# A spectral mixing and SwiGLU kernel: smaller n tiles, three a tiles for four, and a last step of 21 units

## The chip, the core and the metric

The kernel runs on one core of a Trainium2 chip. The core has five engines that run side by side: TensorE (PE in the profile; its weight loads are shown apart as PEld), VectorE (DVE), ScalarE (ACT), GpSimd (POOL) and SyncE (SP), which here only issues DMA transfers. Each engine works through its own instructions in order and waits on semaphores for the others. Matmul results land in PSUM, eight banks of 128 x 512 fp32; everything else lives in SBUF or in DRAM. The metric is the time of one execution on the device in microseconds, as the median of several runs.

## What is computed

For each of 8 batches of 3008 rows with 256 channels, a Fourier filter along the rows, then a normalisation and a gated feed-forward layer on every row:

```
def _attn_ref(x, filt_r, filt_i):
    X = np.fft.rfft(x, axis=1)
    F = (filt_r + 1j * filt_i)[None, :, :]
    y = np.fft.irfft(X * F, n=x.shape[1], axis=1)
    return y.astype(np.float32)

def _moe_ref(x, w_gate, w_val, w_out, rms_g):
    rms = np.sqrt(np.mean(x * x, axis=-1, keepdims=True) + 1e-06)
    xn = x / rms * rms_g
    g = xn @ w_gate
    silu = g * (1.0 / (1.0 + np.exp(-g)))
    return (silu * (xn @ w_val) @ w_out).astype(np.float32)
```

Here d_ff is 1536. The feed-forward layer holds most of the arithmetic: 24,064 rows times three matrices of 256 x 1536.

## The kernel before

**Two kinds of work.** The row index of a batch is split as 94 x 32, and the Fourier transform and its inverse are done as matmuls in three stages with layout changes through DRAM between them. For a batch b these are: `load_x`; `s1` (16 pieces i, each a matmul into PSUM `psa` and a copy into the tile `a_sb`; every four pieces fill one a tile of 8 rows, which SyncE writes to `a_tmp`, line 153); `load_a2`; `s2` and `s2z` (12 pieces j: filter and second transform, tiles `z_sb`, written to `z_tmp`); `load_z2`; and the last step, 16 pieces q of two rows each. A piece q of the last step is `s3` (a matmul into `psy`, and two squares with a sum on ScalarE, line 256), `s3r` (two operations on GpSimd that give rho, the factor 1/rms, lines 265 and 267) and `s3n` (VectorE multiplies the PSUM result by rho into the tile `n_sb`, line 276). Every four pieces fill one n tile of 8 rows, which SyncE writes to `n_tmp` (line 280). Then `load_xn` reads n back transposed, one chunk of up to 512 rows at a time, by transposing DMAs on SyncE (line 318). A chunk takes rows from all n tiles of its batch, so its read waits for all writes of n.

The feed-forward layer is cut in units. A unit is one chunk of rows and one of twelve blocks of 128 hidden channels: two matmuls for the gate (`pg`, line 341), two for the value (`pv`, line 345), a silu on ScalarE (`sg`, line 348) and a product on VectorE (`hh`, line 350). `project` follows three units behind and adds the output matmuls into `po` (line 364); after the twelfth block it copies `po` out and SyncE writes it (line 381 in batch 0, line 389 later). Batch 0 has 8 chunks of 376 rows, units 0 to 95; each later batch has 6 chunks, 72 units.

**The order.** It is written out by hand. `plan` holds, for each unit number (slot), which pieces are issued right after that unit's matmuls, those of `s3n` first, then `s3r`, `s2z` and the rest (line 469); after them comes `project` of three units before. So the transform of batch b runs inside the units of the batch before it. For each batch `o_s3` is the slot of the first piece of the last step: 63 for batch 1, and 31 units ahead of the batch's own units for the others. Piece q is in slot `o_s3 + q + q // 2` for batch 1 and `o_s3 + q + q // 4` for the others; its `s3r` is one slot later, its `s3n` two. The six `load_xn` of a batch start three slots after the last `s3`. For batch 1 that puts `s3` of q = 15 in slot 85, its `s3n` in slot 87 and the first `load_xn` in slot 88; unit 96 is the first that uses it.

**Before unit 0.** The transform of batch 0 goes another way (`s1_first`, `turn`, no a tile), and the part ahead of the units ends as follows (lines 568 to 588): SyncE loads the first half of z of batch 0 and four pieces of the weights; `s1` of batch 1 runs its pieces 0 to 11, whose copies alternate between ScalarE and VectorE; then come four matmuls and eight squares of `s3` for batch 0, and pieces 12 to 15 of `s1`, all four copied by VectorE (line 151); then `s3n_first(0)`, in which VectorE scales the first rows of n (line 287), and `turn_n`, which transposes them on TensorE and evicts them into `xn`, so that unit 0 can start. On VectorE the order is thus: the four copies of pieces 12 to 15, then the scalings.

**Tiles and buffers.** A tile with a tag takes the next of `bufs` buffers, and the first instruction that writes it waits until all users of that buffer's earlier tile are done, DMA writes included. `a_sb` has four buffers of 8 x 256 fp16 per partition, `n_sb` two of the same size. PSUM is one pool of eight banks for all stages.

Of the kernel before, what the change touches and what calls it, by code (L numbers as in the profile page):

```python
# [11 lines left out]
FP16 = mybir.dt.float16  # L12
# [5 lines left out]
D = 256  # L18
# [7 lines left out]
PY = 96  # L26
QZ = 4 * NS
# [47 lines left out]
def kernel(  # L75
# [11 lines left out]
    nc = tc.nc  # L87
# [10 lines left out]
    n_dram = nc.dram_tensor("n_tmp", (B, PY, RP, D), FP16, kind="Internal").ap()  # L98
    n0_dram = nc.dram_tensor("n0_tmp", (RP // 4, PY, 4, D), FP16, kind="Internal").ap()

    glob = ctx.enter_context(tc.tile_pool(name="glob", bufs=1))
    work = ctx.enter_context(tc.tile_pool(name="work", bufs=2))
    psum = ctx.enter_context(tc.tile_pool(name="psum", bufs=8, space=bass.MemoryType.PSUM))

    def bank(name):
        return psum.tile([P, 512], FP32, tag="bank", name=name)
# [32 lines left out]
    def s1(b, i, eng):  # L139
        v = st[b]  # L140
        if i % 4 == 0:
            v.a = work.tile([QZ, 8, D], FP16, tag="a_sb", name="a_sb", bufs=4)
        ps = bank("psa")
        nc.tensor.matmul(ps[0:QZ, :], w1_sb, v.x[i // 4][:, ds(2 * (i % 4), 2), :],  # L144
                         start=True, stop=True)
        dst = v.a[:, ds(2 * (i % 4), 2), :]
        src = ps[0:QZ, :].rearrange("p (r d) -> p r d", r=2)
        if eng == 0:
            nc.scalar.activation(out=dst, in_=src, func=AXT.Copy)  # L149
        else:  # L150
            nc.vector.tensor_copy(out=dst, in_=src)
        if i % 4 == 3:
            nc.sync.dma_start(
                a_dram[b].rearrange("s c r d -> (s c) r d")[:, ds(8 * (i // 4), 8), :], v.a)
# [116 lines left out]
    def s3n(b, q):  # L271
        v = st[b]
        ps, rho = v.y.pop(q)
        if q % 4 == 0:
            v.n = work.tile([PY, 8, D], FP16, tag="n_sb", name="n_sb", bufs=2)
        nc.vector.tensor_tensor(out=v.n[:, ds(2 * (q % 4), 2), :],  # L276
                                in0=ps[0:PY, :].rearrange("p (r d) -> p r d", r=2),
                                in1=rho.unsqueeze(-1).to_broadcast([PY, 2, D]), op=ALU.mult)
        if q % 4 == 3:
            nc.sync.dma_start(n_dram[b, :, ds(8 * (q // 4), 8), :], v.n)  # L280

    def s3n_first(c):
        v = st[0]
        n = work.tile([PY, 8, D], FP16, tag="n_sb", name="n0", bufs=2)
        for k in range(2):
            ps, rho = v.y.pop(2 * c + k)
            nc.vector.tensor_tensor(out=n[:, ts(k, 2), :],
                                    in0=ps[0:PY, :].rearrange("p (r d) -> p r d", r=2),
                                    in1=rho.unsqueeze(-1).to_broadcast([PY, 2, D]), op=ALU.mult)
        if c >= PRE:  # L290
            nc.sync.dma_start(n0_dram[c], n[:, 0:4, :])
        return n

    def turn_n(c, n):
# [141 lines left out]
    def at(slot, f, *args):  # L436
        plan.setdefault(slot, []).append((f, args))

    for c in range(PRE, RP // 4):
        k = 2 + 8 * (c - PRE)  # L440
        at(k, s3, 0, 2 * c, 2)
        at(k + 1, s3, 0, 2 * c + 1, 2)
        at(k + 2, s3r, 0, 2 * c, 2)
        at(k + 4, s3n_first, c)
        at(k + 7, load_xn_first, c)

    for b in range(1, B):
        end = FIRST + UNITS * (b - 1)
        o_s1 = 44 if b == 2 else end - 118
        o_s2, p_s2 = (14, 3) if b == 1 else (end - 75, 2)  # L450
        o_s3 = 63 if b == 1 else end - 31
        if b > 1:
            at(o_s1 - 18, load_x, b)
            for i in range(16):
                at(o_s1 + i, s1, b, i, i % 2 if b == 2 else 0)
            at(o_s1 + 16, load_a2, b)
        for j in range(12):
            k = o_s2 + p_s2 * j
            at(k, s2, b, j)
            at(k + (3 if b < 2 else 5), s2z, b, j)  # L460
        at(k + (4 if b < 2 else 6), load_z2, b)
        for q in range(16):
            k = o_s3 + q + (q // 2 if b == 1 else q // 4)
            at(k, s3, b, q)
            at(k + 1, s3r, b, q)
            at(k + 2, s3n, b, q)
        for c in range(6):
            at(k + 3 + c, load_xn, b, c)
# [62 lines left out]
    with tc.manual_schedule():  # L531
# [40 lines left out]
        for i in range(12):  # L572
            s1(1, i, i % 2)
# [4 lines left out]
        for i in range(12, 16):  # L578
            s1(1, i, 1)
        load_wo(1)  # L580
        load_wo(2)
        n0 = s3n_first(0)
        turn_n(0, n0)
        load_w(4)
        n1 = s3n_first(1)
        at(2, turn_n, 1, n1)
        load_z2(0, 16, 16)
# [44 lines left out]
```

## Time and profile before

| | us |
|---|---|
| median of 3 runs | 901.75 (901.72 to 901.91) |
| the profiled execution | 903.26 |
| its span, first to last instruction | 901.4 |
| VectorE busy | 646.3 |
| ScalarE busy | 640.3 |
| GpSimd busy | 336.5 |

The profile is of one execution. Its times are in microseconds from the first instruction. A row of the timeline gives the start, the length, engine, line, operation, the tiles written and read, the shapes and how many were merged; in brackets stands how long the engine was idle before, and what ended that. A row of the chain of waits gives start, length and what the end of the kernel was waiting for then. Rows of SyncE (SPq) are issues of DMAs, not the transfers; for these the profile has the time from issue to landing. A row of windows gives, for a stretch, its length, how long each engine was busy with how many instructions, the clock that TensorE was granted as a share of full speed, the busy share of the DMA engines and the data rate. Matmul ends are modelled, so matmuls that follow each other overlap in the rows.

### The profile page before, as it was taken

The numbers are of one execution on the slowest core, as the hardware profiler recorded it, in microseconds if no ns is written. First come the engines' busy times: TensorE is split into PE (matmuls) and PEld (weight loads), VectorE is DVE, ScalarE is ACT, GpSimd is POOL, SyncE is SP. The second block draws the span as 40 slices with busy tenths as digits, with TensorE's granted clock in tenths as the row PEclk, the third lists the DMA queues.
The fourth block names the chain that finished last, engine by engine and source line by source line (L and its number), as shares of the span: only waits on it lengthen the run. The fifth ranks groups of instructions, "written<-read, shape, count | busy, mean of one in ns | idle before, by whom it ended". The sixth has DMA issues, their size and how long they took to land.

```text
span 901.4 us, 16402 instructions
## 1 busy us (share of the span) xinstructions
PE 865.6 (96%) x5528; PEld 550.1 (61%) x5528; DVE 646.3 (72%) x1026; ACT 640.3 (71%) x1455; POOL 336.5 (37%) x438
## 2 busy tenths in 40 slices
PE   5669999999999999999999999999999999999998
PEld 4336776666556655666556665566656666565565
DVE  4668887796578947797477965789467985865554
ACT  5556768687886778677886878867786775854543
POOL 3822104492245803285044921459033750400000
PEclk9769999999999999999999999999999999999999
DMA  8996675465436555344655554365553425250111
GB/s 205 239 265 148 163 162 184 114 151 132 140 100 142 133 147 168 97 110 129 164 147 128 134 127 147 111 131 145 146 159 96 101 76 118 77 130 24 35 37 45
DMA packets 140812, 117.30 MB, mean 130 GB/s; under 512 B 53976, under 2 KB 125272, under 8 KB 140728
## 3 DMA queue, kind: packets, MB, share of 16 engines
q1 hardware_dynamic: 136248, 102.13, 42.2%
q0 software_dynamic: 4240, 13.90, 8.7%
q8 instruction: 43, 0.70, 0.3%
q14 instruction: 41, 0.34, 0.1%
q10 hardware_dynamic: 240, 0.23, 0.1%
HBM read 56.96 MB, written 60.42 MB: 130 GB/s over the span
## 4 chain that ended last, share of the span: by engine, by line
PE 85%; DMA 5%; ACT 4%; DVE 2%; issue 2%; POOL 1%; SPq 0%; DVEq 0%; ACTq 0%; POOLq 0%
PE po L364 25%; PE pv L345 25%; PE pg L341 25%; PE psy L250 3%; ACT junk L256 2%; PE psa L144 2%; PE psz L229 2%; PE psp L200 2%; DMA z<-z_tmp 2%; ACT sg L348 1%; DMA w_sb<-w0tab 1%; DMA z_tmp<-z_sb 1%; DVE t L208 1%; DMA fr_sb<-in_filt_r_dram 1%; DMA n_tmp<-n_sb 0%
## 5 line engine op out<-in xcount | busy, mean ns | idle before, releaser
L350 DVE TENSOR_TENSOR hh<-pv,sg 128x512 f16<-128x512 f32 (+2 forms) x600 | 393.3, 658 | 221.3 <-ACT sg L348 129.8
L348 ACT ACTIVATE sg<-pg 128x512 f32<-128x512 f32 (+2 forms) x600 | 341.0, 568 | 198.4 <-PE pg L341 161.4
L364 PE MATMUL po<-wo_sb,hh 128*128 128x256 f16 (+1 forms) x2288 | 347.9, 272 | 0.2 <-DVE n_sb L276 0.2
L345 PE MATMUL pv<-xn,wv_sb 128*128 128x512 f16 (+2 forms) x1200 | 343.0, 367 | 4.6 <-ACT sg L348 3.8
L341 PE MATMUL pg<-xn,wg_sb 128*128 128x512 f16 (+2 forms) x1200 | 343.1, 367 | 3.1 <-DMA xn<-n_tmp 1.9
L364 PEld LDWEIGHTS <-hh 128*128 128x128 f16 (+1 forms) x2288 | 233.2, 104 | 102.7 <-DVE n_sb L276 0.5
L345 PEld LDWEIGHTS <-wv_sb 128*128 128x128 f16 x1200 | 117.5, 98 | 133.5 <-issue 6.6
L265 POOL TENSOR_SCALAR me<-ms 96x2 f32<-96x2 f32 (+1 forms) x120 | 26.1, 217 | 347.3 <-ACT junk L256 340.3
L341 PEld LDWEIGHTS <-wg_sb 128*128 128x128 f16 x1200 | 117.4, 98 | 16.8 <-DMA xn<-n_tmp 2.1
L217 POOL TENSOR_TENSOR pi<-pi,fi_sb 64x512 f32<-64x512 f32 x72 | 91.2, 1267 | 71.3 <-ACT pi L214 67.8
L256 ACT ACTIVATE junk<-psy 96x256 f16<-96x256 f32 x256 | 97.0, 379 | 20.6 <-PE psy L250 8.6
L218 POOL TENSOR_TENSOR qq<-pr,pi 128x512 f16<-128x512 f32 x72 | 91.6, 1272 | 10.6 <-DVE pi L216 5.0
L267 POOL TENSOR_TENSOR rho<-me,half_sb 96x2 f32<-96x2 f32 (+1 forms) x120 | 87.5, 729 | 10.0
L276 DVE TENSOR_TENSOR n_sb<-psy,rho 96x512 f16<-96x512 f32 x112 | 75.8, 677 | 0.0
L234 ACT ACTIVATE z_sb<-psz 128x512 f16<-128x512 f32 x96 | 57.3, 597 | 10.2 <-PE psz L232 5.9
L149 ACT ACTIVATE a_sb<-psa 96x512 f16<-96x512 f32 x94 | 55.6, 591 | 7.1 <-PE psa L144 3.4
L250 PE MATMUL psy<-z,t_sb 96*96 96x512 f16 x128 | 49.5, 391 | 6.8 <-DMA z<-z_tmp 6.8
L216 DVE TENSOR_TENSOR pi<-psp,fi_sb 64x512 f32<-64x512 f32 x72 | 49.9, 693 | 1.9
L215 DVE TENSOR_TENSOR pr<-psp,fr_sb 128x512 f32<-128x512 f32 x72 | 49.6, 689 | 0.7
L256 ACT ACTIVATION_READ_ACCUMULATOR junk<-psy 96x1 f32 x256 | 49.0, 191 | 0.0
L214 ACT ACTIVATE pi<-psp 64x512 f32<-64x512 f32 x72 | 42.4, 588 | 6.1
L144 PE MATMUL psa<-xt,w_sb 94*96 94x512 f16 x112 | 44.2, 417 | 1.6 <-DMA xt<-in_x_dram 1.6
(57 smaller groups left out, 386.7 us busy)
## 6 DMA issues: line engine op xcount, KB each, us to landing
out_dram<-o SPq DMA_DIRECT2D x70, 256.0 KB, 2.5
z_tmp<-z_sb SPq DMA_DIRECT2D x32, 384.0 KB, 2.3
xt<-in_x_dram POOLq DMA_DIRECT2D x32, 376.0 KB, 7.2
a_tmp<-a_sb SPq DMA_DIRECT2D x28, 384.0 KB, 3.6
a<-a_tmp SPq DMA_DIRECT2D x28, 384.0 KB, 5.8
z<-z_tmp SPq DMA_DIRECT2D x7, 1536.0 KB, 10.0
n_tmp<-n_sb SPq DMA_DIRECT2D x28, 384.0 KB, 3.0
out_dram<-o SPq DMA_DIRECT2D x12, 224.0 KB, 2.6
```

Source lines behind the costliest of these rows:

```text
L144: nc.tensor.matmul(ps[0:QZ, :], w1_sb, v.x[i // 4][:, ds(2 * (i % 4), 2), :], start=True, stop=True)
L217: nc.gpsimd.tensor_tensor(out=pi[64:P], in0=pi[64:P], in1=fi[64:P], op=ALU.mult)
L218: nc.gpsimd.tensor_tensor(out=qq, in0=pr, in1=pi, op=ALU.subtract)
L250: nc.tensor.matmul(ps[0:PY, :], t_sb, v.z2[:, ts(q, 2), :], start=True, stop=True)
L256: nc.scalar.activation(out=junk, in_=ps[0:PY, ts(i, D)], func=AXT.Square, scale=0.0625, accum_out=v.ms[:, ds(k + i, 1)])
L267: nc.gpsimd.tensor_tensor(out=rho, in0=me, in1=half_sb[:, 0:2 * pair], op=ALU.pow)
L276: nc.vector.tensor_tensor(out=v.n[:, ds(2 * (q % 4), 2), :], in0=ps[0:PY, :].rearrange("p (r d) -> p r d", r=2), in1=rho.unsqueeze(-1).to_ ...
L341: nc.tensor.matmul(pg[:, 0:w], wg_sb[:, dt_, ts(jt, P)], xn[:, dt_, 0:w], start=(dt_ == 0), stop=(dt_ == 1))
L345: nc.tensor.matmul(pv[:, 0:w], wv_sb[:, dt_, ts(jt, P)], xn[:, dt_, 0:w], start=(dt_ == 0), stop=(dt_ == 1))
L348: nc.scalar.activation(out=sg[:, 0:w], in_=pg[:, 0:w], func=AXT.Silu)
L350: nc.vector.tensor_tensor(out=hh[:, 0:w], in0=pv[:, 0:w], in1=sg[:, 0:w], op=ALU.mult)
L364: nc.tensor.matmul(po[0:n, ts(0 if alone else s4 % 2, D)], hh[:, ds(s4 * wb, n)], wo_sb[:, jt, :], start=(jt == 0 and (s4 % 2 == 0 or alone)),
```

## The change

Three edits. The tag `n_sb` gets six buffers of four rows in place of two of eight: a tile is allocated at every second piece q and written to DRAM after the next one, so a batch issues eight writes of 192 KB in place of four of 384 KB; batch 0's own n tile has four rows, all used. The tag `a_sb` gets three buffers in place of four, so that a batch's fourth a tile takes a buffer that has been used three tiles earlier. The SBUF taken by both together stays the same (12 KB and 12 KB per partition in place of 8 and 16). And the sixteen pieces of batch 1's last step have one free slot after every third in place of every second: slots 63 to 83 in place of 63 to 85, with `s3r`, `s3n`, the writes of n and the six `load_xn` moved with them (first `load_xn` in slot 86 in place of 88).

```diff
@@ s1
-            v.a = work.tile([QZ, 8, D], FP16, tag="a_sb", name="a_sb", bufs=4)
+            v.a = work.tile([QZ, 8, D], FP16, tag="a_sb", name="a_sb", bufs=3)
@@ s3n
-        if q % 4 == 0:
-            v.n = work.tile([PY, 8, D], FP16, tag="n_sb", name="n_sb", bufs=2)
-        nc.vector.tensor_tensor(out=v.n[:, ds(2 * (q % 4), 2), :],
+        if q % 2 == 0:
+            v.n = work.tile([PY, 4, D], FP16, tag="n_sb", name="n_sb", bufs=6)
+        nc.vector.tensor_tensor(out=v.n[:, ds(2 * (q % 2), 2), :],
...
-        if q % 4 == 3:
-            nc.sync.dma_start(n_dram[b, :, ds(8 * (q // 4), 8), :], v.n)
+        if q % 2 == 1:
+            nc.sync.dma_start(n_dram[b, :, ds(4 * (q // 2), 4), :], v.n)
@@ s3n_first
-        n = work.tile([PY, 8, D], FP16, tag="n_sb", name="n0", bufs=2)
+        n = work.tile([PY, 4, D], FP16, tag="n_sb", name="n0", bufs=6)
...
-            nc.sync.dma_start(n0_dram[c], n[:, 0:4, :])
+            nc.sync.dma_start(n0_dram[c], n)
@@ the plan
-            k = o_s3 + q + (q // 2 if b == 1 else q // 4)
+            k = o_s3 + q + q // (3 if b == 1 else 4)
```

## The prediction

> **What bounds the kernel now.** I read the busy times first, then who waits for whom, then the chain of waits around the two places that the change touches, and last the timeline there, engine by engine.
>
> ```profile
> PE 865.6 (96%) x5528; PEld 550.1 (61%) x5528; DVE 646.3 (72%) x1026; ACT 640.3 (71%) x1455; POOL 336.5 (37%) x438
> ```
>
> TensorE (PE) is busy for 865.6 of 901.4 us. So only 36 us of the span are open to a change of order, and any later start of the feed-forward part is paid almost in full, because after it TensorE hardly pauses. The view of waits, of which two rows matter here, says where it does:
>
> ```profile
> PE pv L345 <- ACT sg L348: 3.8, 5, 0.8
> ...
> PE pg L341 <- DMA xn<-n_tmp: 1.9, 1, 1.9
> ```
>
> The second is one wait of 1.9 us: the first unit of the second batch (unit 96) wants the transposed n of that batch. The chain of waits shows its pieces (start, length, what), and the timeline of TensorE the idle time in brackets:
>
> ```profile
> 167.51 4.16 DMA n_tmp<-n_sb
> ...
> 171.75 3.65 DMA xn<-n_tmp
> ```
> ```profile
> 175.45 0.61 PE L341 MATMUL pg<-xn,wg_sb 128*128 128x512 f16 x2 [1.85 <-DMA xn<-n_tmp]
> ```
>
> The last write of n to DRAM (4.16 us, issued once VectorE has scaled its rows), the transposing read (3.65 us), then TensorE, idle for 1.85 us. TensorE would have been ready at 175.45 - 1.85 = 173.60. That idle time is what the shorter step (21 units for 24) can win. The other place is the start of the feed-forward part. These are rows of SyncE's queue, of the DMA issued there, of VectorE, GpSimd and TensorE:
>
> ```profile
> 46.86 7.23 SPq L153 DMA_DIRECT2D a_tmp<-a_sb  x4
> ```
> ```profile
> L153 SPq DMA_DIRECT2D a_tmp<-a_sb x1: 652/652/652, 46.9 to 46.9; - x1
> ...
> DMA to landing us min/median/max: 7.2/7.2/7.2
> ```
> ```profile
> 51.27 2.48 DVE L151 CAST a_sb<-psa 96x512 f16<-96x512 f32 x4 [8.15 <-PE psa L144]
> 53.68 1.27 DVE L287 TENSOR_TENSOR n<-psy,rho 96x512 f16<-96x512 f32 x2
> ```
> ```profile
> 51.95 1.05 POOL L267 TENSOR_TENSOR rho<-me,half_sb 96x4 f32<-96x4 f32 x1
> ```
> ```profile
> 56.46 0.79 PE L341 MATMUL pg<-xn,wg_sb 128*128 128x376 f16 x2 [0.79 <-ACT xn L304]
> ```
>
> VectorE copies the second batch's fourth a tile (four casts from 51.27), then at once scales the first n (53.68), whose factor rho was ready at 51.95 + 1.05 = 53.00. From there runs the path to unit 0: transposes of n on TensorE, their eviction by ScalarE (xn, the releaser in the last row), first matmul at 56.46. So the four casts stand directly ahead of the critical path, without slack: n starts when they end.
>
> **The change part by part.** *Three a tiles in place of four.* The second batch is the first to use a tiles (batch 0 goes another way), so its fourth tile is a new buffer before and the first tile's buffer after. The first cast into it must then wait until the write of that first tile has left it. That write was issued at 46.86, behind the z loads and four weight loads on SyncE, and landed 7.2 us later, at 54.06. The DMAs ahead of it on SyncE and the casts that feed them are untouched by the change, so the cast starts at 54.06 in place of 51.27: **+2.79 us**. Behind it on VectorE stand the three other casts and the two scalings of n; for these wait the transposes, ScalarE's eviction and unit 0, all with no cover. On SyncE the write of the fourth tile, four weight loads, one z load and the loads of a stand behind those casts and start as much later, as do the units that use them; I count nothing more for them. Bounds: a release that takes as long to be seen as the one from landing to transposing read in the chain (171.75 - 167.51 - 4.16 = 0.08) adds 0.1, the rounding of 7.2 takes or adds 0.05. I take 2.79, from 2.7 to 2.9; that there is no wait at all is a rival below.
>
> The clock then decides what the later start costs. The windows view of TensorE (stretch, length, busy, granted clock, DMA share, GB/s):
>
> ```profile
> 48.70:52.12 3.42, 3.23 (x8) 0.50 1.02 328
> ...
> 55.53:58.95 3.42, 2.63 (x11) 0.50 0.93 241
> 58.95:62.36 3.41, 3.41 (x18) 0.50 1.01 217
> 62.36:65.77 3.41, 3.41 (x27) 1.00 1.15 234
> ```
>
> Unit 0 runs at half clock, and full clock is granted at 62.36, after the first stretch that is wholly busy; 3.23 of 3.42 at 48.70 was not enough. After the change unit 0 starts at 56.46 + 2.79 = 59.25, inside the stretch 58.95 to 62.36, which is then about 3.1 busy, less than the 3.23 that failed. If stretches lie where they did, the clock rises one later, at 65.77: the half-clock part lasts 65.77 - 59.25 = 6.52 in place of 62.36 - 56.46 = 5.90 us, and half of the 0.62 is lost: +0.3. I take +0.2, from 0 (small waits of TensorE just behind may swallow it) to 0.3. The Trainium skill (TensorE: Matmul & The Clock Gate, Part 1: The HAM clock gate) says that the clock rises after a busy window of about 3.4 us, and that these windows run freely, unaligned to the kernel. By its free-running grid alone, the next edge inside the run being enough, the clock would still rise at 62.36 here; this is the first rival below.
>
> Later batches use the three tiles too. There the first tile is written nine units ahead of the fourth tile's first copy. The tile's view gives the slowest write of a from the third batch on (215 to 665 us), the list of DMAs the median of all, and of the 192 KB writes of n in the first batch:
>
> ```profile
> DMA to landing us min/median/max: 3.0/4.5/7.9
> ```
>
> ```profile
> a_tmp<-a_sb SPq DMA_DIRECT2D x28, 384.0 KB, 3.6
> ...
> n_tmp<-n SPq DMA_DIRECT2D x6, 192.0 KB, 2.2
> ```
>
> No unit is shorter than 0.97 us (rows below), so nine are 8.7 us, against 7.9 at most and 3.6 in the median: no wait. If that cover were gone, ScalarE's copies would be held for the remainder of a write, 7.9 us at worst, and TensorE for what its banks don't cover.
>
> *The second batch's last step in 21 units.* The sixteen steps q start at unit 63 + q + q/3 in place of 63 + q + q/2, so the last scaling moves from unit 87 to 85 and the first transposing read from 88 to 86. The pace of TensorE, the lag of VectorE and what else stood on SyncE:
>
> ```profile
> 159.70 0.48 PE L341 MATMUL pg<-xn,wg_sb 128*128 128x376 f16 x2
> ...
> 160.67 0.48 PE L341 MATMUL pg<-xn,wg_sb 128*128 128x376 f16 x2
> ...
> 161.85 0.48 PE L341 MATMUL pg<-xn,wg_sb 128*128 128x376 f16 x2
> ```
> ```profile
> 162.58 0.68 DVE L276 TENSOR_TENSOR n_sb<-psy,rho 96x512 f16<-96x512 f32 x1
> ```
> ```profile
> 159.95 0.32 SPq L280 DMA_DIRECT2D n_tmp<-n_sb  x1
> 164.65 2.76 SPq L381 DMA_DIRECT2D out_dram<-o  x3
> ```
>
> A unit without the step takes 0.97 us (unit 83, 159.70 to 160.67), one with it 1.18 (unit 84): 0.21 for its matmul. In the old time scale, with all sixteen steps now ahead of unit 84, that unit starts at 160.67 + 2 x 0.21 = 161.09 and unit 85 at 162.06. The scaling of unit 84 began at 162.58, 1.91 after its unit; so the last one begins at 163.97 and ends at 164.65. Its write now holds four rows, 192 KB, and is issued ahead of the three output writes of unit 86, not behind them. It lands after 2.2 us (the 192 KB row) to 4.16 (the chain's): 166.9 to 168.8. The read adds 0.08 + 3.65: 170.6 to 172.5, ahead of 173.60. **The 1.85 us of idle time goes whole**, with 1.1 us or more to spare; in the new time scale both sides shift alike. The three output writes then queue behind that read on SyncE, some 4 us later than their 164.65. The tiles they empty are wanted again twelve units on, over 11 us, so nobody waits.
>
> What the denser step costs is the open term. In these units ScalarE does one silu and two squares:
>
> ```profile
> 158.45 0.38 ACT L256 ACTIVATE junk<-psy 96x256 f16<-96x256 f32 x1
> ...
> 159.32 0.47 ACT L348 ACTIVATE sg<-pg 128x376 f32<-128x376 f32 x1
> 159.69 0.37 ACT L256 ACTIVATE junk<-psy 96x256 f16<-96x256 f32 x1
> ```
> ```profile
> 152.00:162.00 10.00, 10.00 (x71) 7.00 (x69) 8.09 (x16) 8.68 (x32) 5.56 (x12) 1.00 0.38 113
> ```
>
> With its queue full, a step and a silu take 159.69 - 158.45 = 1.24 us, 0.06 more than TensorE's unit of 1.18; a free unit gives back 0.97 - 0.47 = 0.50. Three in a row fall 0.18 behind and the fourth unit recovers it: 4 units need 3 x 1.24 + 0.47 = 4.19 on ScalarE and 3 x 1.18 + 0.97 = 4.51 on TensorE. VectorE (8.09 of 10) and GpSimd (5.56) have room: the steps per unit rise from 2/3 to 3/4 only. So ScalarE stays just under TensorE, 93%. Not shown is whether eight PSUM banks are enough when three step results are in flight. One row is near: at a chunk boundary in this stretch, where the banks are shortest, TensorE already lost 0.22 us.
>
> ```profile
> 151.69 0.32 PE L364 MATMUL po<-wo_sb,hh 128*120 128x256 f16 x1 [0.22 <-DVE n_sb L276]
> ```
>
> The later batches run four in a row and pay 0.75 or 0.8 once each (first row of the waits above, 3.8 over 5). I take 0, being nearest to the ScalarE sum; from -0.2 (the loss at the boundary goes) to +1.4 (five groups at 0.18 unrecovered, and 0.75 in place of 0.22 at the boundary: 0.90 + 0.53).
>
> *n in six tiles of four rows.* The scaling itself is unchanged. Each batch issues eight writes of 192 KB for four of 384, 28 more in all, at about 0.32 us of SyncE each (row 159.95). They go where SyncE waits for VectorE anyway. Six tiles of four hold 24 rows in flight where two of eight held 16, so no new wait; from the third batch on the reads have slack of ten units, so the smaller last write wins nothing there. In the first batch a tile of eight rows was only ever half used, and now fits. I take 0; if SyncE had no idle time, 4 x 0.32 = 1.3 us a batch would lie on outputs, not on TensorE.
>
> The sum: 2.79 + 0.2 - 1.85 + 0 = +1.14, rounded to **+1.1 us**. The profiled execution took 903.26 us, of which the span is 901.4 and 1.86 lie around it; it becomes 902.5 in span. The median of the runs is 901.75, 1.5 below the profiled time, and the same step gives **902.85**.
>
> **The rivals.** *The clock hides half of the late start.* If full clock comes at 62.36 in spite of the later start, only 62.36 - 59.25 = 3.11 us are slow in place of 5.90, which gives back 1.4: 2.79 - 1.40 - 1.85 = -0.46, so 901.3. Against it: the failed stretch at 48.70. Chance 0.12.
>
> *The fourth tile does not wait*, because the buffer is let go sooner than the landing says, or the casts find another way past it: then only the gain is left, 901.75 - 1.85 = 899.9, and without the boundary's loss 899.7. The point is whether the first cast starts below 51.5. For it: nothing in the trace; it is the case where half of the change does not do what it says. Chance 0.09.
>
> *The denser step binds*: banks run short with three results in flight, so units 65 to 83 lose up to the 1.4 worked out above while the wait at unit 96 is gone anyway: 902.85 + 1.4 = 904.25. It decides the sign of the second edit from 1.85 us of new idle time in these units. For it: the 0.22 and 0.75 us; against it: ScalarE's 93%. Chance 0.2.
>
> **How the numbers follow.** The forecast has 0.59, the rest 0.12, 0.09 and 0.2. Within 0.2% of 901.75 is within 1.8 us, about what a measurement of this kernel can tell from no change. The forecast and the clock rival lie inside it but for a tail of 0.05 above; the waitless tile is just faster; the dense step is slower in most of its range (0.16 of 0.2). That makes faster 0.09, same 0.70, slower 0.21. The forecast alone spans 902.3 (2.7, no cost of the clock, -0.2 from the step: +0.65, rounded down) to 903.8 (2.9, 0.3, and half of the step's 1.4); to leave out no more than 2 in 10, the range goes from 900.4 to 904.5.
>
> **What would show it.** The first cast of the fourth a tile near 54.1 with a DMA as releaser, unit 0 near 59.25, full clock at 65.8 (or 62.4 for the first rival); no wait of TensorE for xn at unit 96 and the first read ending over 1 us ahead; the units 63 to 84 near 24 us. I am wrong if the cast starts at 51.3, if the stretch of the denser step shows over 0.5 us of new idle time, or if the time leaves 900.4 to 904.5.

## The result, and the profile after

| | before | after |
|---|---|---|
| median of 11 runs, us | 903.05 (901.72 to 904.22) | 899.73 (898.48 to 901.78) |
| profiled execution, us | 903.26 | 900.67 |
| its span, us | 901.4 | 898.8 |

The ratio is 0.9967 with a 95% interval of 0.9957 to 0.9976: the change makes the kernel faster by 0.33%, 3.0 us (the two medians differ by 3.3). The forecast was 1.1 us slower. The eleven runs of before reach higher than the three shown ahead of the prediction.

Three places differ between the two profiles. First the start of the feed-forward part. These are VectorE's and TensorE's rows of the timeline after, and the time to landing of the first write of an a tile:

```profile
55.58 2.48 DVE L151 CAST a_sb<-psa 96x512 f16<-96x512 f32 x4 [11.50 <-DMA a_tmp<-a_sb]
57.98 1.27 DVE L287 TENSOR_TENSOR n<-psy,rho 96x512 f16<-96x512 f32 x2
```
```profile
60.76 0.79 PE L341 MATMUL pg<-xn,wg_sb 128*128 128x376 f16 x2 [0.79 <-ACT xn L304]
```
```profile
L153 SPq DMA_DIRECT2D a_tmp<-a_sb x1: 681/681/681, 47.5 to 47.5; - x1
...
  DVE a_sb L151: 11.5, 1
...
DMA to landing us min/median/max: 7.9/7.9/7.9
```

The casts now wait for the DMA, as forecast, and unit 0 starts at 60.76 in place of 56.46, 4.3 us late. Of this 0.4 us is no part of the change: z came that much later in this execution, as the part on the prediction shows.

Second, unit 96. SyncE's rows and TensorE's:

```profile
165.49 3.20 SPq L280 DMA_DIRECT2D n_tmp<-n_sb  x2
170.47 1.89 SPq L318 DMA_TRANSPOSE xn<-n_tmp  x1
172.45 2.23 SPq L381 DMA_DIRECT2D out_dram<-o  x3
```
```profile
177.20 0.59 PE L341 MATMUL pg<-xn,wg_sb 128*128 128x512 f16 x2
```

No bracket at 177.20: the wait of 1.85 us is gone, and the first read was issued 6.7 us ahead. The lateness is 177.20 - 175.45 = 1.75 us here.

Third, what the forecast had no term for. TensorE's waits of before held five of 0.75 us that ended with a silu. Of the rows of waits after, the ones for `pg` and `pv` are these, and none is left that ends with `sg`:

```profile
PE pg L341 <- ACT xn L304: 0.8, 1, 0.8
PE pv L345 <- DVE t L208: 0.7, 1, 0.7
```

One of the five before, at unit 151, as TensorE's and ScalarE's rows show it, and then the same unit after:

```profile
257.59 0.59 PE L341 MATMUL pg<-xn,wg_sb 128*128 128x512 f16 x2
258.94 0.59 PE L345 MATMUL pv<-xn,wv_sb 128*128 128x512 f16 x2 [0.75 <-ACT sg L348]
```
```profile
258.31 0.58 ACT L348 ACTIVATE sg<-pg 128x512 f32<-128x512 f32 x1
```
```profile
259.34 0.59 PE L341 MATMUL pg<-xn,wg_sb 128*128 128x512 f16 x2
259.77 0.59 PE L345 MATMUL pv<-xn,wv_sb 128*128 128x512 f16 x2
260.20 0.60 PE L364 MATMUL po<-wo_sb,hh 128*128 128x256 f16 x4
```
```profile
260.05 0.58 ACT L348 ACTIVATE sg<-pg 128x512 f32<-128x512 f32 x1
```

Before, the value matmuls of a unit wait until the silu of the same unit (258.31 + 0.58 = 258.89) has read the gate result. By the algorithm they have nothing to do with each other. (The gate result is `pg`, the value result `pv`.) After, ScalarE is just as late (the silu comes 0.71 us after the unit's first matmul, before 0.72), and the value matmuls run ahead of it. The reason stands in the two programs as they are built, in the PSUM bank that each result is given:

```
unit        before: pg  pv  psy      after: pg  pv  psy
149                  0   5   1               4   3   5
150                  3   0   5               1   4   3
151                  3   3   -               2   1   -
152                  6   0   7               4   6   2
```

In unit 151 of the kernel before, gate and value share bank 3, and so again in units 223, 295, 367 and 439; after, no unit has both in one bank. From unit 96 to unit 599 the profiled execution takes 719.02 us before (175.45 to 894.47) and 714.43 after (177.20 to 891.64). That is 4.6 us, 0.92 for each of the five, and no other unit of this stretch differs by more than a few hundredths.

### The profile page after: what moved, and what is told of

Read it like the earlier page. It is cut to its first block, busy times and chain, and to the rows that moved or that the text cites. A ratio compares the mean times of both kernels' runs of the same rounds, so it can differ in the third digit from the quotient of the medians.

```text
span 898.8 us, 16487 instructions
## 1 busy us (share of the span) xinstructions
PE 863.3 (96%) x5528; PEld 549.1 (61%) x5528; DVE 646.5 (72%) x1026; ACT 640.6 (71%) x1455; POOL 336.5 (37%) x438
## 4 chain that ended last, share of the span: by engine, by line
PE 90%; DMA 3%; DVE 2%; ACT 1%; issue 1%; SPq 0%; POOL 0%; DVEq 0%; ACTq 0%; POOLq 0%
PE po L364 27%; PE pv L345 27%; PE pg L341 27%; PE psy L250 3%; PE psa L144 2%; PE psz L229 2%; PE psp L200 2%; DMA xt<-in_x_dram 1%; DMA a_tmp<-a_sb 1%; DMA z_tmp<-z_sb 1%; ACT junk L256 1%; DMA fr_sb<-in_filt_r_dram 1%; DVE t L208 1%; DVE hh L350 0%; PE psz L232 0%
```

## Experiments

Ratios are against the kernel before on the same chip, with the 95% interval. Theory A is that the five waits went because more rows of n are in flight, theory B that the denser step shifted the banks.

**The denser step alone.** The last edit of the diff, without the others.

> Only the denser last step of the second batch (21 units), n and a tiles as before. Theory A (the five later waits go because of the rows of n in flight): units 0 to 62 as before, the wait at unit 96 gone, 2.2 us less at unit 96, and the five waits of 0.75 us of the later batches stay: about 2.2 us faster than before, 0.9975. Theory B (they go because the denser step shifts every later turn of the PSUM banks): the five waits are gone too, 6.8 us faster, 0.9925.

Measured: 0.9987 (0.9978 to 0.9996). The wait at unit 96 is gone and the five waits are there:

```profile
PE pv L345 <- ACT sg L348: 3.8, 5, 0.8
```

B is out. By the ratio the step alone is worth 1.2 us (0.4 to 2.0), less than the 2.2 expected.

**The denser step with three a tiles.** The kernel above with

```diff
-            v.a = work.tile([QZ, 8, D], FP16, tag="a_sb", name="a_sb", bufs=4)
+            v.a = work.tile([QZ, 8, D], FP16, tag="a_sb", name="a_sb", bufs=3)
```

> Denser step and three a tiles, n in two tiles of eight rows as before. Theory A: unit 0 starts 4 us late as in the changed kernel, the wait at unit 96 is gone, the five waits of 0.75 us are back: 1.8 us slower than before, 1.002. Theory B: the five waits are gone, 2.8 us faster like the changed kernel, 0.997.

Measured: 1.0014 (1.0006 to 1.0023), with the five waits. The casts wait for the DMA here too, and unit 0 starts 2.2 us later than with the step alone. The rows are this kernel's first cast, then its first matmuls on z and its unit 0, then the same two of the step alone:

```profile
53.79 2.48 DVE L151 CAST a_sb<-psa 96x512 f16<-96x512 f32 x4 [11.18 <-DMA a_tmp<-a_sb]
```
```profile
47.30 1.91 PE L250 MATMUL psy<-z,t_sb 96*96 96x512 f16 x4 [5.42 <-DMA z<-z_tmp]
...
58.97 0.79 PE L341 MATMUL pg<-xn,wg_sb 128*128 128x376 f16 x2 [0.79 <-ACT xn L304]
```
```profile
49.20 1.91 PE L250 MATMUL psy<-z,t_sb 96*96 96x512 f16 x4 [6.32 <-DMA z<-z_tmp]
...
56.76 0.79 PE L341 MATMUL pg<-xn,wg_sb 128*128 128x376 f16 x2 [0.79 <-ACT xn L304]
```

The 2.2 us flatter the change: z came 1.90 us earlier in this execution than in that of the step alone. Counted from the first matmul on z, unit 0 starts after 11.67 us here and after 7.56 there, 4.1 us apart. By the ratios the third a tile's loss is 1.0014 - 0.9987 = 0.0027, 2.4 us. This kernel is the change without its n tiles, and it is slower than before, as the forecast said of the whole.

**n tiles and three a tiles, the step in 24 units.** The diff without its last edit.

> n in six tiles of four rows and three a tiles, the second batch's last step in 24 units as before. Theory A: unit 0 starts 4 us late, the wait of about 1.9 us at unit 96 stays or shrinks with the smaller last write, the five waits of 0.75 us (0.92 us a unit) are gone: 4.0 - 4.6 = 0.6 us faster than before, 0.9993. Theory B: the five waits stay, 4 us slower, 1.0044.

Measured: 0.9974 (0.9963 to 0.9985); the five waits are gone. And the wait at unit 96 went as well, without the denser step:

```profile
167.25 2.76 SPq L381 DMA_DIRECT2D out_dram<-o  x3
170.10 0.49 SPq L280 DMA_DIRECT2D n_tmp<-n_sb  x1
172.83 2.62 SPq L318 DMA_TRANSPOSE xn<-n_tmp  x2
```
```profile
176.19 0.60 PE L341 MATMUL pg<-xn,wg_sb 128*128 128x512 f16 x2
```

The last write, still behind the three output writes, took 2.7 us for its 192 KB where before it took 4.16 for 384. So the small tiles cover most of what the denser step covers.

**24 rows of n in three tiles of eight.** In the kernel before:

```diff
-            v.a = work.tile([QZ, 8, D], FP16, tag="a_sb", name="a_sb", bufs=4)
+            v.a = work.tile([QZ, 8, D], FP16, tag="a_sb", name="a_sb", bufs=3)
...
-            v.n = work.tile([PY, 8, D], FP16, tag="n_sb", name="n_sb", bufs=2)
+            v.n = work.tile([PY, 8, D], FP16, tag="n_sb", name="n_sb", bufs=3)
...
-        n = work.tile([PY, 8, D], FP16, tag="n_sb", name="n0", bufs=2)
+        n = work.tile([PY, 8, D], FP16, tag="n_sb", name="n0", bufs=3)
```

> n in three tiles of eight rows (24 rows in flight, writes of 384 KB as before), three a tiles, last step in 24 units. If the rows of n in flight decide the banks, the five waits are gone as with six tiles of four; unit 0 is late by 3 to 4 us and the wait of 1.9 us at unit 96 is back, since the last write is large again: about 1 us faster than before, 0.999. If the small tiles decide, the five waits stay and the kernel is 3 to 4 us slower than before, 1.004.

Measured: 0.9991 (0.9982 to 1.0000). The five waits are gone and the one at unit 96 is back:

```profile
179.16 0.60 PE L341 MATMUL pg<-xn,wg_sb 128*128 128x512 f16 x2 [1.82 <-DMA xn<-n_tmp]
```

**16 rows of n in four tiles of four.** The changed kernel with four buffers for n and four for a:

```diff
-            v.a = work.tile([QZ, 8, D], FP16, tag="a_sb", name="a_sb", bufs=3)
+            v.a = work.tile([QZ, 8, D], FP16, tag="a_sb", name="a_sb", bufs=4)
...
-            v.n = work.tile([PY, 4, D], FP16, tag="n_sb", name="n_sb", bufs=6)
+            v.n = work.tile([PY, 4, D], FP16, tag="n_sb", name="n_sb", bufs=4)
...
-        n = work.tile([PY, 4, D], FP16, tag="n_sb", name="n0", bufs=6)
+        n = work.tile([PY, 4, D], FP16, tag="n_sb", name="n0", bufs=4)
```

> n in four tiles of four rows (16 rows in flight as before), four a tiles, last step in 21 units. If the rows in flight decide, the five waits stay and unit 0 is on time: 1 to 2 us faster than before like the denser step alone, 0.9985. If the small tiles decide, the five waits are gone: 6 us faster, 0.993.

Measured: 0.9994 (0.9985 to 1.0003), less of a gain than the 1 to 2 us expected. Unit 0 is on time at 56.60, the waits read again

```profile
PE pv L345 <- ACT sg L348: 3.8, 5, 0.8
```

These two settle it: the five waits follow the rows in flight, 24 against 16, not the size of a tile or of a write. Nor is it the number of tiles: three of eight rows have no such wait, four of four rows have all five.

**One bank again.** The changed kernel, with the shared bank put back by hand in the five units. For this the silu of these units stands ahead of the value matmuls in the program, and the units behind them are given other banks too (unit 152 has 1 and 4 in place of 4 and 6); all else is as it was:

```diff
-        pv = bank("pv")
+        sg = work.tile([P, 512], FP32, tag="sg", name="sg", bufs=3)
+        same = JT * g + jt in (151, 223, 295, 367, 439)
+        if same:
+            nc.scalar.activation(out=sg[:, 0:w], in_=pg[:, 0:w], func=AXT.Silu)
+        pv = pg if same else bank("pv")
...
-        sg = work.tile([P, 512], FP32, tag="sg", name="sg", bufs=3)
-        nc.scalar.activation(out=sg[:, 0:w], in_=pg[:, 0:w], func=AXT.Silu)
+        if not same:
+            nc.scalar.activation(out=sg[:, 0:w], in_=pg[:, 0:w], func=AXT.Silu)
```

> The changed kernel, but at units 151, 223, 295, 367 and 439 the value matmuls are put into the bank of the gate matmuls of the same unit, so that they must wait for the silu. If the shared bank is the whole of the five waits of 0.75 us (0.92 us a unit), they come back at these units: 4.6 us slower than the changed kernel, 1.002 against the kernel before. If the waits had another cause that the change removed (ScalarE less late, other DMAs), the five units lose clearly less than 0.9 us each.

Measured: 1.0033 (1.0020 to 1.0045), 6.0 us slower than the changed kernel's 0.9967; the intervals reach down to 4.0 and so cover the 4.6. In the profile the wait is back in its old size, here under the name `pg`, whose bank the value matmuls write:

```profile
261.13 0.59 PE L349 MATMUL pg<-xn,wv_sb 128*128 128x512 f16 x2 [0.76 <-ACT sg L346]
```

From unit 96 to 599 it takes 719.03 us (177.64 to 896.66), as before the change, and of all units in this stretch only the five differ from the changed kernel by more than a few hundredths, by 0.92 us each.

**The step of batches 2 to 7 one unit earlier**, in the kernel before:

```diff
-        o_s3 = 63 if b == 1 else end - 31
+        o_s3 = 63 if b == 1 else end - 32
```

> The kernel before, with the last step of batches 2 to 7 one unit earlier (32 units ahead in place of 31). The program's banks then put gate and value of one unit into the same bank at units 150, 222, 294, 366 and 438 in place of 151 and so on. If the shared bank is the wait, the five waits of 0.75 us move to those units and the time stays, 1.000. If the waits come from what stands around the chunk boundary at unit 151, they stay there or change in size.

Measured: 0.9997 (0.9988 to 1.0006). The wait moved with the bank, to unit 150:

```profile
254.49 0.59 PE L341 MATMUL pg<-xn,wg_sb 128*128 128x512 f16 x2
255.83 0.59 PE L345 MATMUL pv<-xn,wv_sb 128*128 128x512 f16 x2 [0.75 <-ACT sg L348]
```

So it does not hang on unit 151 itself, and no chunk boundary lies there: chunks begin at units 144 and 156. The step moved as well, so this run alone does not part bank and step; one_bank_again does.

**The late start.** The changed kernel with the four casts behind the first scaling of n:

```diff
-        for i in range(12, 16):
-            s1(1, i, 1)
         load_wo(1)
         load_wo(2)
         n0 = s3n_first(0)
         turn_n(0, n0)
+        for i in range(12, 16):
+            s1(1, i, 1)
```

> The changed kernel with the four casts of the fourth a tile (and their matmuls) put behind the first scaling of n and its transposes. If the wait for the a tile's buffer is what makes unit 0 late, unit 0 starts near 56 in place of 60.8, and the kernel is 4 to 5 us faster than the changed one, some 7 us faster than before: 0.992. If the late start comes from the loads ahead of it, unit 0 stays near 60 and the time like the changed kernel's, 0.997.

Measured: 0.9946 (0.9930 to 0.9962), unit 0 at 55.95:

```profile
55.95 0.83 PE L341 MATMUL pg<-xn,wg_sb 128*128 128x376 f16 x2
```

It beats the kernel before by 4.9 us and the changed one by 0.0021, 1.9 us, where the intervals still touch; 4 to 5 us were expected. Of the earlier start a part is given back at unit 3, where TensorE waits for the first products behind the casts on VectorE:

```profile
62.78 0.27 PE L364 MATMUL po<-wo_sb,hh 128*120 128x256 f16 x1 [1.25 <-DVE hh L350]
```

Two of the casts on ScalarE were meant to mend that:

> As casts_behind_n, with two of the four casts on ScalarE. VectorE is free 1.2 us sooner for the first product: the wait of 1.25 us of TensorE at 62.8 there shrinks to nothing or little, 0.5 to 1 us faster than casts_behind_n, 0.994 against the kernel before. If ScalarE's two casts delay the first silu, it is no faster than casts_behind_n.

Measured: 0.9937 (0.9924 to 0.9949); the wait at unit 3 is still 1.16 us, so the expectation failed, and this kernel and casts_behind_n can't be told apart by time. This interval lies wholly below that of the changed kernel (0.9957 to 0.9976): with the casts behind n, two of them on ScalarE, the kernel does beat both. With the step back in 24 units:

> casts_behind_n with the last step of the second batch in 24 units as before. Since the smaller last write alone took the wait at unit 96 away in n_and_a, the denser step should be worth nothing or a few tenths: unit 96 within 0.5 us of casts_behind_n as counted from unit 9, 0.994 to 0.995. If the denser step is what pays, unit 96 is 2 us later and the time 0.997.

Measured: 0.9950 (0.9935 to 0.9964), not to be told from casts_behind_n by time, with 0.81 us of wait at unit 96. Counted from unit 9, unit 96 comes 0.75 us later than there, a little more than the half microsecond expected. And the order alone, in the kernel before:

> The kernel before (four a tiles, no wait for a buffer) with the four casts behind the first scaling of n. Unit 0 starts about 0.7 us earlier than before, since n no longer stands behind the casts: 0.999. If the casts then only block the first products, nothing is won: 1.000.

Measured: 1.0001 (0.9991 to 1.0011). Unit 0 did not come earlier: counted from the first matmul on z, it starts after 7.63 us here and after 7.56 in the kernel before. VectorE scales n sooner, but the four matmuls that feed the casts now stand directly ahead of unit 0 on TensorE, which is busy without a pause:

```profile
50.50 1.91 PE L250 MATMUL psy<-z,t_sb 96*96 96x512 f16 x4 [6.92 <-DMA z<-z_tmp]
...
56.43 1.91 PE L144 MATMUL psa<-xt,w_sb 94*96 94x512 f16 x4
58.13 0.83 PE L341 MATMUL pg<-xn,wg_sb 128*128 128x376 f16 x2
```

Without a late buffer the order is worth nothing that these runs can tell; it pays as the cure of the third a tile.

## Why the prediction was wrong

**The step that failed is "n in six tiles of four rows ... I take 0".** The forecast looked for the cost of the small tiles in queues and buffers of n, found none, and stopped there. The edit was worth 0.9967 - 1.0014 = -0.0047, 4.2 us by the ratios of the changed kernel and of the one without its n tiles, and 4.6 us by the profiles from unit 96 on. It works through another resource: with 24 rows of n in flight instead of 16, the program gives PSUM banks in another order, and five units no longer put gate and value in one bank.

**The row was there and was misread.** "The later batches run four in a row and pay 0.75 or 0.8 once each" took the five waits as the price of a busy ScalarE, a fixed cost of the dense step, and used them only to bound batch 1. The trace of before told more: the silu that ended the wait was of the same unit. The value matmuls need nothing from the silu of their own unit, unless they have to write the bank that it reads; a ScalarE that is merely late would hold them at the bank of an older unit. Of the bank question itself the forecast said "not shown is whether eight PSUM banks are enough" for the denser step, and did not ask it of the edit that changed when they come free.

**Three a tiles: right mechanism, too small a size.** The forecast had 2.79 us, from 2.7 to 2.9. The casts did wait for that write. But z comes at another time in each execution, and the start of unit 0 moves with it: in the thirteen profiles the first matmul on z starts at 47.30 to 50.50. These are the rows of before and after:

```profile
48.90 1.91 PE L250 MATMUL psy<-z,t_sb 96*96 96x512 f16 x4 [6.50 <-DMA z<-z_tmp]
```
```profile
49.27 1.91 PE L250 MATMUL psy<-z,t_sb 96*96 96x512 f16 x4 [5.92 <-DMA z<-z_tmp]
```

Counted from there, unit 0 starts after 7.6 us in all four profiles with four a tiles and the old order of the casts, and after 11.4 to 12.0 in the five with three: 3.8 to 4.5 us late, in the changed kernel 60.76 - 49.27 = 11.49 against 56.46 - 48.90 = 7.56, that is 3.9. The forecast took the landing from one trace, 5.2 us after that first matmul (54.06 - 48.90), and its narrow bounds from there too; in the five kernels that wait for it the same write landed 6.0 to 6.7 us after. The ratios give 2.4, with intervals that allow 0.9 to 4.1.

**The clock.** Forecast +0.2, on the premise that the stretches lie where they did. They don't. TensorE's windows after, in the same columns as those of before:

```profile
57.55:60.96 3.41, 1.20 (x9) 0.50 1.06 228
60.96:64.38 3.42, 3.42 (x12) 0.50 0.96 332
64.38:67.79 3.41, 2.80 (x24) 1.00 1.15 224
```

Full clock came 64.38 - 60.76 = 3.6 us after unit 0, against 5.9 before. That is a gain, not a loss, but a small one: at unit 9 the changed kernel is still 4.0 us late (72.35 against 68.34). The edges sit at 64.38 here and at 62.36 before. In the trace of before the granted clock also changes at 21.40 and 35.05, where these windows begin:

```profile
17.98:21.40 3.42, 3.42 (x28) 0.50 0.93 227
21.40:24.81 3.41, 2.83 (x30) 1.00 1.08 232
...
35.05:38.46 3.41, 2.47 (x6) 0.50 1.02 231
```

From 21.40 to 35.05 and from there to 62.36 it is 4 and 8 times 3.41 us, so the next edge of before would lie at 62.36 + 3.41 = 65.77, and 64.38 is no multiple away: the grid is not tied to the kernel's start. That is what the Trainium skill says of it (TensorE: Matmul & The Clock Gate, Part 1: The HAM clock gate), and these traces agree. So this term is drawn anew in each execution, and neither its +0.2 nor the rival's -1.4 was a forecast of the median. The 5.9 us of before were themselves an outlier: in the twelve other profiles full clock came 2.5 to 4.1 us after unit 0.

**The denser step.** The wait at unit 96 went whole, as worked out: with one write of 192 KB at the end and the first read issued 6.7 us ahead. Unit 95, which holds that wait, takes 1.18 us in place of 3.20. The step's own cost, put at 0, was 0.50 in units 64 to 86 (26.54 us against 26.04), most of which the units behind give back: up to the start of unit 95 it is 34.47 against 34.29. So the step gains 1.8 us by these profiles. But its gain depends on what stands beside it: with the new n tiles, which shorten the same wait, units 64 to 95 take 35.65 us with and without the denser step. The ratios, 1.2 us with the old n tiles and 0.9974 - 0.9967 = 0.0007 or 0.6 us with the new ones, can't tell the two apart. The rival of the denser step that binds is out, and so is the fourth tile that does not wait.

**The sum**, by ratios in the order in which the edits were put together: step -1.2, third a tile +2.4, n tiles -4.2, together -3.0 us. As a chain of differences it adds up by construction. By the profiles the same terms are -1.8, +3.9 and -4.6, together -2.5, where the two spans differ by 2.6. Of the three, the n tiles turn the sign: without them the kernel is 1.3 us slower than before, where the forecast had 1.1 for the whole. That these agree is in part luck: by the profiles the third a tile costs 1.1 us more than its term.

**What stays open.** That the rows in flight set the banks is shown by the two kernels with 24 and 16 rows, and that the shared bank is the wait by putting it back. Why 16 rows lead to a shared bank is argued only: the banks are given when the program is made, it seems in an order of time that is assumed there, and with 16 rows piece 8 of a step has to follow the write of an earlier n tile, so its bank would be counted free later. The trace of before shows no scaling of n on VectorE held by such a write. That the shared unit moved by one with the step fits this, but no run tested it by itself. Open too is why the third a tile costs less by the ratios than by the profiles.

## What to carry to other kernels

When a matmul waits for an engine that reads the result of the unit it belongs to, compare the PSUM banks of the two: a shared one is a choice of the program, and any edit that moves buffers, even of another tile, can make it or undo it. So give an edit of buffer counts a term for the banks, and where the banks can be listed, list them for both programs before costing anything else. And where a buffer is taken from a tile with idle buffers, look at its first use, when the writes that free it stand in the longest queue, and put what is not urgent behind what the next stage waits for.

## What the runs showed of the hardware

The stretch from unit 96 to unit 599 repeats to a few hundredths of a microsecond between kernels that have the five waits, and between those that have none: 719.02, 719.02 and 719.03 us for the kernel before, the denser step alone and one_bank_again, 714.43 and 714.45 for the changed kernel and n_three_of_eight. That points to the part ahead of unit 96, with its loads from DRAM and the changes of the clock, as the place of most of the spread of the timed runs (901.72 to 904.22); the arrival of z alone moved by 3.2 us between the profiles (47.30 to 50.50). A change inside that stretch can be read from one profile to 0.1 us, where the medians need 1.
